# Seven half-size products for the first matrix product of two more groups, with a new schedule

## Chip, cores, metric

The kernel runs on one core of a Trainium2 chip. The metric is device microseconds from start to end of one execution. Three runs of the kernel before gave 276.33, 275.78 and 276.13 us: median **276.13 us**.

## What is computed

Linear attention with a positional weighting, and behind it a two-layer network with leaky ReLU. With B = 8 batches, H = 8 heads, S = 576 positions, D = 64:

```python
c, s = cos(pi/2 * pos/S), sin(pi/2 * pos/S)
phi(x) = concat(relu(x) * c, relu(x) * s)          # 128 features
kv  = einsum('bhsf,bhsd->bhfd', phi(k), v)
num = einsum('bhsf,bhfd->bhsd', phi(q), kv)
den = phi(q) . sum_s phi(k) + 1e-6
x   = (num / den) as 4608 tokens x 512
h   = x @ w_in                                      # 512 -> 2048
out = leaky_relu(h, 0.01) @ w_out                   # 2048 -> 512
```

Inputs and output are float32; the kernel multiplies in float16 and accumulates in float32.

## The kernel before, in words

**Groups.** The tokens go through the network in nine groups of 512: group g = 0 to 7 holds the first 512 positions of batch g, and group 8 the last 64 positions of all eight batches. For each group the kernel forms phi(q) (`q_prep`, tiles qp), transposes it by DMA (`q_transpose_dma`, qpT, line 363), and multiplies it with the batch's kv in four steps (`num`, line 400; PSUM pool ps_n with one buffer, which kv_sum uses too). Each num is divided on VectorE (DVE): den and its reciprocal (lines 411 and 415) and the product (line 416) into xs; line 377 then transposes the whole group by DMA into xT. Attention for batch b needs phi(k) (`k_cos` and `k_sin`, nine half-tiles each, written kp below, lines 251 on ScalarE (ACT) and 253 on DVE or GpSimd (POOL); kp has one buffer), v with a column of ones (`v_pairs`, vm), and `kv_sum` (72 small matmuls at line 326 and a copy on ACT at line 333).

**First product.** h = x @ w_in in two ways. *Direct* (`ffn1`, line 474, units "M"): 16 column blocks of 128, each four matmuls of 512 columns; ACT applies the leaky ReLU to two blocks at once (line 484, 128x1024). *By seven* (`ffn1s`, line 626, digits 1 to 7): the matrices are cut into 2 x 2 blocks, and seven products of half size stand for eight (Winograd's form of Strassen's scheme). A group has four units u, each of seven products, each of four matmuls of 256 columns. It needs sums of blocks of the weights (`w1_sum`, W sums in tile wext, once) and of x (`x_sum`, X sums, per group; n = 3 in place). The products of a unit accumulate in three of four PSUM banks, A, E and B. `ffn1e` moves between them: b copies A to B after product 1, s and u copy E and B aside, z adds u to E, y adds s to B (both on DVE, line 526), and a, c, e, d are four leaky ReLUs (ACT, line 653). Capital letters B, S, U put a copy on DVE. The fourth bank lets a unit begin while the last one is read; a unit's B and E are banks that the unit before releases through its e and a.

**Second product.** out = g @ w_out, by seven from group 1 on (`ffn2s`, line 737, units "F"): 14 parts, each of two half-units of four matmuls of 256 columns. Its block sums of g are `g_sum` (S1, S2 in tile ext; n = 3, 4 in place), those of w_out `weight_sum` (T), all on DVE. The results leave as osb on DVE or ACT and are stored from SyncE's queue (SP, line 796). Group 0's results are held and stored later (`store_held`, line 809).

**Order.** From batch 2 on, the order is written out in the table TUNE. Time is counted in units: stage g, positions 16g to 16g+16, holds ffn2 of group g and ffn1 of group g+1. `O[g+1]` is the order of the matmul units in that stage, spread evenly over it; everything else stands at a position, and each engine executes in that order. For batch b: `L` loads of q, k and v, `q`, `kc`, `ks`, `v` the phi and v steps with engines `e` (D, A, P; S is a POOL tensor_scalar in place of a cast), `qT` and `x` the two kinds of transposes, `mm` kv_sum and `n` the four nums. `S` and `S4s` are g sums, `W`, `X` and `T` the other sums, with engines `We` and `Xe`.

**Buffers.** Loads take a ring of four staging buffers (`stage_tile`), some of them tiles wext and ext: wext holds a quarter of w_in, then k of batch 1, then k of batch 3, before the W sums may use it. All loads, transposes and most stores are issued from SP in program order, so one that waits holds those behind it.

Seven-product ffn1 is in use for groups 4 to 8 (`F7 = 4`); groups 0 to 3 are direct.

Of the kernel before, what the change touches and what calls it, by code (L numbers as in the profile page):

```python
# [16 lines left out]
T = 9  # L17
# [3 lines left out]
def kernel(  # L21
# [15 lines left out]
    B, H, S, D = q.shape  # L37
# [12 lines left out]
    NG = B + 1  # L50
    NE = D + 2
    G7 = 1
    F7 = 4

    ctx.enter_context(tc.manual_schedule())

# [31 lines left out]
    def need(*keys):  # L88
        for key in keys:
            assert key in done, key  # L90
# [8 lines left out]


    wext = const.tile([P, 3080], dt.float32, name="wext")
    in_wext = {("w1", 1), ("k", 1), ("k", 3)}

    def stage_tile(nm, i, a, b, d):
        if (nm, i) in in_wext:
# [43 lines left out]
    w1 = {}  # L149
# [95 lines left out]
    kv = [const.tile([P, H, NE], dt.float16, name=f"kv{b}") for b in range(B)]  # L245
# [319 lines left out]
        )  # L565

    def w1_sum(bp, n, eng):
        need(("kv", 3), *(("W", bp, i) for i in {1: (), 2: (1,), 4: (2,), 3: (1,)}[n]))
        if n == 3:
            need(*(("f1", F7 - 1, 8 * bp + 4 + i) for i in range(4)))  # L570
        done.add(("W", bp, n))
        a11, a12, a21, a22 = (w1_quarter(bp, r, d) for r in range(2) for d in range(2))
        o1, o2, o4 = (SW[i][:, bp] for i in (1, 2, 4))
        if n == 1:
            tt_op(o1, a21, a22, ALU.add, eng)
        elif n == 2:
            tt_op(o2, o1, a11, ALU.subtract, eng)
        elif n == 3:
            tt_op(a21, a11, a21, ALU.subtract, eng)
        else:  # L580
            tt_op(o4, a12, o2, ALU.subtract, eng)
# [223 lines left out]
    held = []  # L805
# [24 lines left out]
    for hg in range(2):  # L830
        for j in range(J):
            e = ACT if j == 3 else POOL if hg == 1 and j == 2 else DVE
# [158 lines left out]
    for m in range(6):  # L991
# [4 lines left out]
    units = []  # L996

    TUNE = {'B': {2: {'L': None,
               'e': 'DDPDAPDDDAPPPDAPAPDDDADP',
               'kc': [13.8758, 13.8602, 13.7361, 13.8137, 13.7827, 13.8913, 13.7206, 14.2749, 13.7516],  # L1000
               'ks': [13.9533, 13.9378, 13.9068, 13.9223, 13.8292, 13.7671, 13.9844, 13.7051, 13.6896],
               'mm': 16.1999,
               'n': [17.3726, 19.1324, 20.1999, 21.6217],
               'q': [10.2124, 10.3249, 10.4374, 10.6624],
               'qT': [13.8447, 13.9689],
               'v': [10.5499, 13.5965],
               'x': 21.7526},
           3: {'L': [10.7749, 13.5654, 13.643, 19.8363],
               'e': 'AADDPAPAAADAAAAAPDAPPDAP',
               'kc': [18.9921, 17.2908, 19.2259, 23.109, 18.3817, 21.589, 20.6044, 16.9272, 21.5563],  # L1010
               'ks': [20.1181, 20.5226, 21.7199, 20.5635, 19.0389, 17.209, 19.0856, 20.6454, 20.4817],
               'mm': 23.4726,
               'n': [24.1999, 26.3817, 27.4726, 28.1454],
               'q': [19.1791, 20.6863, 15.7749, 22.6635],
               'qT': [20.9272, 22.7454],
               'v': [21.5235, 21.6544],
               'x': 28.2544},
           4: {'L': [16.5635, 25.2363, 22.8272, 22.8272],
               'e': 'PPAPDADDDPDDDAPADAAPPPPA',
               'kc': [36.3363, 36.0635, 37.2908, 33.1926, 33.3235, 38.7999, 28.5635, 36.2544, 37.6544],  # L1020
               'ks': [36.1181, 37.7363, 38.6908, 35.4181, 36.1726, 36.309, 36.0908, 38.3817, 36.9272],
               'mm': 38.9999,
               'n': [39.7817, 41.2581, 42.4144, 43.4726],
               'q': [21.7854, 22.3817, 33.2581, 34.3817],
               'qT': [28.6454, 36.1454],
               'v': [25.6544, 32.5963],
               'x': 43.7817},
           5: {'L': [33.6544, 32.9817, 36.2272, 36.2272],
               'e': 'ADADADADPDAADDDPPAADDAPA',
               'kc': [39.1635, 46.3272, 40.9817, 50.1825, 50.3564, 45.9363, 39.109, 46.0181, 45.6872],  # L1030
               'ks': [42.2835, 41.3235, 39.0544, 49.9695, 44.9817, 40.8726, 50.0086, 51.9216, 46.4363],
               'mm': 52.9651,
               'n': [53.6608, 55.9216, 55.0856, 58.1564],
               'q': [39.2181, 43.8908, 42.349, 45.2363],
               'qT': [44.8726, 50.7434],
               'v': [50.6651, 43.3908],
               'x': 58.7042},
           6: {'L': [41.389, 46.0999, 52.2695, 52.2695],
               'e': 'PPDAPAADPAPAPAPDDDADAPAD',
               'kc': [55.7086, 58.2086, 60.8173, 62.3042, 60.9495, 55.7869, 62.3303, 61.4869, 54.9962],  # L1040
               'ks': [55.0185, 60.9182, 60.7651, 57.139, 55.0409, 61.0121, 55.0633, 61.8086, 54.5303],
               'mm': 64.9495,
               'n': [66.9042, 68.5782, 70.7042, 74.5042],
               'q': [55.108, 59.0521, 55.7477, 61.8608],
               'qT': [59.1999, 64.4042],
               'v': [58.5303, 61.139],
               'x': 74.7042},
           7: {'L': [58.3564, 62.4086, 65.0121, 65.0121],
               'e': 'APPAAPDAAPAADPPAPAPAPPDA',
               'kc': [69.9695, 77.4869, 73.6999, 67.9216, 70.0477, 64.9808, 74.7434, 68.6173, 69.8608],  # L1050
               'ks': [78.7199, 65.9825, 70.8782, 69.3129, 78.6886, 65.4608, 73.6216, 69.8086, 68.6564],
               'mm': 81.0121,
               'n': [81.4869, 84.0956, 85.4869, 87.026],
               'q': [64.4434, 64.9182, 68.2695, 74.5564],
               'qT': [74.1825, 80.9025],
               'v': [75.0521, 76.6173],
               'x': 89.4869},
           8: {'L': [66.0347, 80.9182, 80.9495, 84.8173],
               'e': 'DAPD',
               'kc': [],  # L1060
               'ks': [],
               'mm': 10.1345,
               'n': [92.7912, 99.0521, 101.8347, 104.0956],
               'q': [80.9964, 84.7651, 85.139, 90.0086],
               'qT': [85.8347, 97.4869],
               'v': [],
               'x': 104.7912}},
     'O': {1: 'MMMMMMMMMM',
           2: 'FFFFFFFFFFFFFFFFFFFFFFFFFFFMMMMMMMMMFMMMMMMM',
           3: 'FMMFFFMFMFFFFFFFFFFFFFFMFMMMMMMMFFMFFMFMMFFF',  # L1070
           4: '1b5sFF6u3Fz2Fe1Fb7FFyFa56Uc2sF7ay4dF3FFz4e1FF5bFsdF362cuFz17FyeaFFF5bc64FsuFF3FF7zy2FFdace4d',
           5: '1bF5sFF63uF172Fzebay652uasF74cFy3dFzcF1FFe4b5FF6FsF23dU7azFyFe51FFbsFF23F6uFc47adzycFFFe4dFF',
           6: '1b5F1Fs6FuF327yzFFaFF5e4b2Fsc6FUF3zdF71yaF54eFb6Us32FzdcFaeFFF7y1bF5F6Fc2UF7asyc3F4dFzFe4dFF',
           7: '1b5F6S2F31FUzFeFFbF7a26u5ycF7sFaFyF45F3FFzSFde14bd26Uc3zFFF17eFyb6au25Fa47scy3dcFFFFFzFe4dFF',
           8: '1b5sFFFF2613u7FaFz5eFyFFbc4S6U2FF73ydaFz5c4FdFe1bFsFF632u17zFyFeFabF6Fu5c72s4y3zdaceFFFF4dFF',
           9: 'FFFFFFFFFFFFFFFFFFFFFFFFFFFF'},
     'S': {1: [13.612, 13.6585, 20.2817, 13.7982, 18.0181, 20.4408],
           2: [28.4817, 32.4654, 32.6617, 32.5308, 32.8726, 36.1999],
           3: [43.5544, 45.3454, 52.7912, 46.7454, 46.6635, 50.0477],
           4: [62.7042, 64.4825, 70.0086, 62.3825, 65.3129, 66.8521, 71.9216],  # L1080
           5: [81.0277, 81.1651, 82.8521, 78.6573, 81.1129, 82.9042, 85.6608],
           6: [91.3999, 92.6434, 100.6173, 92.5912, 97.1651, 99.7738, 97.1129],
           7: [108.6173, 113.8086, 117.8608, 113.4608, 113.5129, 113.8608, 117.8086],
           8: [124.939, 124.9912, 130.6856, 126.0086, 130.5142, 131.1713, 131.7428]},
     'S4': 21.6872,
     'S4s': {2: [37.5726, 41.1926],
             3: [59.2521, 60.0956],
             4: [74.6651, 73.6608],
             5: [87.5738, 87.0782],
             6: [106.7042, 103.5738],  # L1090
             7: [124.2695, 121.139]},
     'T': [10.8874, 13.5809, 13.674, 15.2749],
     'W': [[25.3454, 33.389, 36.2817, 42.4799], [35.5272, 39.8908, 40.1999, 50.5303]],
     'We': ['PDDP', 'DDDD'],
     'X': {4: [45.5563, 45.6217, 50.7042, 45.7526],
           5: [60.9808, 62.8782, 65.5129, 62.3564],
           6: [78.7512, 80.9338, 80.9808, 80.9651],
           7: [92.9651, 94.0086, 99.7216, 94.1825],
           8: [108.4434, 109.4869, 115.226, 109.6608]},
     'Xe': {4: 'DDDD', 5: 'PDDD', 6: 'DPDD', 7: 'DPDD', 8: 'PDDP'},  # L1100
     'held': 13.6275}

    for g in range(NG):
        order, seen = TUNE["O"][g + 1], {}
# [101 lines left out]
```

## Time and profile before

| | before |
|---|---|
| median of three runs | 276.13 us |
| the profiled execution, its own time | 276.87 us |
| its span | 275.1 us |
| TensorE (PE) busy, weight loads (PEld) | 266.3 us, 212.5 us |
| DVE, ACT, POOL busy | 201.5, 171.6, 112.2 us |
| bytes moved by DMA | 57.59 MB, 209 GB/s |

By stretches of the profiled execution (us busy):

| stretch, us | PE | PEld | DVE | ACT | POOL | DMA share |
|---|---|---|---|---|---|---|
| 53 to 66: direct ffn1 of group 1 | 13.00 of 13 | 7.06 | 12.93 | 9.58 | 11.34 | 1.12 |
| 66 to 92: ffn2 of group 1, group 2 begins | 24.98 of 26 | 18.98 | 18.38 | 14.12 | 19.53 | 0.95 |
| 92 to 125 | 33.00 of 33 | 22.25 | 23.39 | 23.55 | 17.66 | 1.04 |
| 125 to 160 | 34.77 of 35 | 32.58 | 29.62 | 26.98 | 21.79 | 1.01 |
| 160 to 193 | 32.70 of 33 | 30.73 | 27.62 | 24.61 | 15.08 | 0.70 |
| 225 to 257 | 32.00 of 32 | 30.18 | 23.16 | 20.43 | 2.31 | 0.21 |

How to read it: a line of the costliest groups gives the source line, engine and operation, what is written and read, the tile's shape, the count, then busy time and mean duration of one, then the engine's idle time ahead of them and what ended it. In the chain of waits and the order of time a line begins with start and duration in us. Matmuls overlap each other, so their mean duration is not their price. An engine's own durations overlap too, by about 0.1 us; from start to start is the price in a full queue.

### The profile page before, as it was taken

How to read it: one execution, taken by the hardware profiler on the slowest of the kernel's cores; microseconds unless marked ns; L12 is line 12 of the kernel's file. 1: busy time of each engine (PE TensorE's matmuls, PEld its weight loads, DVE VectorE, ACT ScalarE, POOL GpSimd, SP SyncE). 2: the span in 40 equal slices, each digit the busy share in tenths (PEclk: the TensorE clock that was granted, in tenths of full speed). 3: DMA queues.
4: the chain of work that ended last, by engine and by line, in shares of the span. 5: the costliest groups of instructions: out<-in, count | busy, mean ns of one | idle time of the engine just before them, and what ended most of it. 6: DMA issues, size and time to landing. Idle time of an engine off the chain costs nothing.

```text
span 275.1 us, 6879 instructions
## 1 busy us (share of the span) xinstructions
PE 266.3 (97%) x2813; PEld 212.5 (77%) x2813; DVE 201.5 (73%) x413; ACT 171.6 (62%) x293; POOL 112.2 (41%) x89
## 2 busy tenths in 40 slices
PE   8899999999999999999999999999999999999993
PEld 3575455557875568668999989999999999999983
DVE  4850597799964467888798878798997787667852
ACT  7756447478914476875679988756844565656400
POOL 2586002795679890440397899210510003000000
PEclk9999999999999999999999999999999999999999
DMA  7999999999699999989988997647915142211214
GB/s 223 373 393 411 383 399 370 374 365 231 207 162 245 302 218 254 289 234 231 226 293 125 272 234 208 148 114 159 183 48 128 27 101 67 69 38 40 77 44 111
DMA packets 77119, 57.59 MB, mean 209 GB/s; under 512 B 49312, under 2 KB 65696, under 8 KB 76704
## 3 DMA queue, kind: packets, MB, share of 16 engines
q1 hardware_dynamic: 76480, 56.63, 75.1%
q10 hardware_dynamic: 608, 0.52, 0.6%
q8 instruction: 22, 0.36, 0.5%
q14 instruction: 9, 0.07, 0.1%
HBM read 36.70 MB, written 9.44 MB: 168 GB/s over the span
## 4 chain that ended last, share of the span: by engine, by line
PE 78%; DMA 9%; DVE 5%; SPq 2%; POOL 2%; ACT 1%; issue 1%; ACTq 0%; DVEq 0%
PE ps L737 27%; PE ps_h L474 20%; PE ps_f L626 18%; PE ps_o L500 5%; DMA xT<-xs 4%; DMA kst<-in_k_dram 3%; PE ps_kv L326 2%; PE ps_num L400 2%; DMA qtl<-in_q_dram 2%; PE ps_f L737 1%; DVE ext L526 1%; POOL kp L253 1%; DVE xs L416 1%; SPq L363 1%; PE ps_qt L386 1%
## 5 line engine op out<-in xcount | busy, mean ns | idle before, releaser
L737 PEld LDWEIGHTS <-g 128*128 128x128 f16 x640 | 61.5, 98 | 8.3 <-DVE g L526 0.2
L737 PE MATMUL ps<-w,g 128*128 128x256 f16 x496 | 64.7, 273 | 0.1
L474 PE MATMUL ps_h<-xT,w 128*128 128x512 f16 (+1 forms) x272 | 59.0, 366 | 0.7 <-DMA xT<-xs 0.7
L474 PEld LDWEIGHTS <-w 128*128 128x128 f16 x272 | 30.0, 114 | 21.8 <-issue 0.8
L484 ACT ACTIVATE g<-ps_h 128x1024 f16<-128x1024 f32 x32 | 32.2, 1022 | 23.2 <-PE ps_h L474 23.1
L653 ACT ACTIVATE g<-ps_f 128x512 f16<-128x512 f32 x60 | 34.7, 596 | 12.9 <-DVE ps_f L526 6.2
L626 PEld LDWEIGHTS <-w 128*128 128x128 f16 x320 | 34.7, 114 | 0.8 <-issue 0.2
L626 PE MATMUL ps_f<-xT,w 128*128 128x256 f16 x240 | 34.4, 273 | 0.0
L737 PE MATMUL ps<-T,ext 128*128 128x256 f16 x240 | 31.4, 273 | 0.0
L253 POOL TENSOR_SCALAR kp<-kst,sin_t 128x256 f16<-128x256 f32 x16 | 20.6, 1295 | 21.7 <-PE ps_kv L326 21.7
L737 PEld LDWEIGHTS <-ext 128*128 128x128 f16 x256 | 24.7, 98 | 3.3
L626 PEld LDWEIGHTS <-wext 128*128 128x128 f16 x240 | 26.2, 114 | 1.2 <-issue 0.6
L253 POOL TENSOR_SCALAR qp<-qst,cos_t 128x512 f16<-128x512 f32 (+1 forms) x9 | 18.3, 2030 | 8.3 <-DMA qst<-in_q_dram 4.3
L416 DVE TENSOR_TENSOR xs<-ps_num,rden 128x512 f16<-128x512 f32 x28 | 19.4, 691 | 2.9 <-DMA xT<-xs 2.0
L253 POOL TENSOR_SCALAR kp<-kst,cos_t 128x256 f16<-128x256 f32 (+1 forms) x15 | 19.7, 1313 | 3.5 <-DMA kst<-in_k_dram 3.3
L626 PE MATMUL ps_f<-X,wext 128*128 128x256 f16 x128 | 18.9, 273 | 0.5 <-ACT ps_f L259 0.5
L526 DVE TENSOR_TENSOR osb<-ps,ext 128x512 f32<-128x512 f32 x23 | 15.7, 684 | 4.0 <-PE ps L737 3.4
L253 POOL TENSOR_SCALAR qp<-qst,sin_t 128x512 f16<-128x512 f32 (+1 forms) x9 | 18.3, 2036 | 0.0
L526 DVE TENSOR_TENSOR ext<-g 128x512 f16<-128x512 f16 (+1 forms) x23 | 14.2, 621 | 5.2 <-ACT g L484 3.4
L526 DVE TENSOR_TENSOR ps_f<-ps_f,u 128x512 f32<-128x512 f32 x20 | 13.9, 694 | 5.2 <-PE ps_f L626 2.7
L737 PE MATMUL ps<-ext,g 128*128 128x256 f16 x128 | 17.3, 273 | 0.0
L526 DVE TENSOR_TENSOR y<-ps_f,s 128x512 f32<-128x512 f32 x20 | 13.7, 687 | 3.2 <-PE ps_f L626 1.5
(118 smaller groups left out, 427.7 us busy)
## 6 DMA issues: line engine op xcount, KB each, us to landing
out_dram<-osb SPq DMA_DIRECT2D x32, 256.0 KB, 3.1
qst<-in_q_dram SPq DMA_DIRECT2D x7, 1024.0 KB, 10.3
kst<-in_k_dram SPq DMA_DIRECT2D x5, 1152.0 KB, 8.1
vst<-in_v_dram SPq DMA_DIRECT2D x5, 1152.0 KB, 7.1
w2st<-in_moe_w_out_dram SPq DMA_DIRECT2D x3, 1024.0 KB, 12.7
vst<-in_v_dram SPq DMA_DIRECT2D x4, 576.0 KB, 7.4
ext<-in_moe_w_in_dram SPq DMA_DIRECT2D x4, 512.0 KB, 10.3
kst<-in_k_dram SPq DMA_DIRECT2D x2, 576.0 KB, 8.1
```

What stands on the lines that cost most here:

```text
L253: eng.tensor_scalar(out=o, in0=i, scalar1=0.0, scalar2=col, op0=ALU.max, op1=ALU.mult)
L326: nc.tensor.matmul(ps[:, o, (c - lo) * NE : (c - lo + 1) * NE], lhsT=st["kp", b][sl, c, j, :], rhs=vm[sl, c, j, :], start=(j == 0), stop=( ...
L363: nc.sync.dma_start_transpose(out=qpT_pair(g, jp).rearrange("p o h t -> p (o h) t"), in_=st["qp2", g, jp].rearrange("p o h f -> p (o h f)"),)
L400: nc.tensor.matmul(ps[lo:hi, h // 4, (h % 4) * NE : (h % 4 + 1) * NE], lhsT=qpT[:, h, lo:hi], rhs=kv[b][:, h, :],)
L416: nc.vector.tensor_tensor(out=xs, in0=ps[:, :, 0 : 4 * NE].rearrange("p a (b e) -> p a b e", e=NE)[:, :, :, 0:D], in1=rden.rearrange("p (a ...
L474: nc.tensor.matmul(ps[:, m % 2, lo:hi], lhsT=w1[m // 4, c][0][:, w1[m // 4, c][1], m % 4 : 512 : 4], rhs=xT[:, lo // P : hi // P, c, :], s ...
L484: nc.scalar.activation(st["g", g][:, m - 1 : m + 1, :], ps, AF.Lrelu)
L500: nc.tensor.matmul(st["ps_o", g, tt], lhsT=st["g", g][:, m, tt * P : (tt + 1) * P], rhs=w2[:, m, :], start=(m == 0), stop=(m == NFT - 1),)
L526: eng.tensor_tensor(out=o, in0=a, in1=b, op=op)
L626: nc.tensor.matmul(ps[:, mi * HT : (mi + 1) * HT], lhsT=a[:, c, 2 * r0 + mi : 512 : 4], rhs=b[:, c], start=(n in (1, 5) and mi == 0 and c ...
L653: nc.scalar.activation(st["g", g][:, m : m + 2, r * HT : (r + 1) * HT], {"a": A, "c": y22, "e": E, "d": B_}[e].rearrange("p (m t) -> p m t ...
L737: nc.tensor.matmul(ps[:, tt], lhsT=a[:, i, tt * P : (tt + 1) * P], rhs=b[:, i], start=(first and i == 0), stop=(i == NPR - 1 and (apart or ...
```

## The change

Groups 2 and 3 also take the seven-product form (`F7 = 2`). The W sums may then begin once kv of batch 1 is summed, and wext no longer holds k of batch 3, which takes a staging buffer. The two g sums of groups 2 and 3 are cut as those of the later groups are. TUNE is replaced from batch 2 on: its core follows, with the lines for batches 2 and 3, the first stages and the first sums; positions, engines and orders for all later batches are other numbers of the same kind.

```diff
-    F7 = 4
+    F7 = 2
...
-    in_wext = {("w1", 1), ("k", 1), ("k", 3)}
+    in_wext = {("w1", 1), ("k", 1)}
...
     def w1_sum(bp, n, eng):
-        need(("kv", 3), ...
+        need(("kv", 1), ...
...
     TUNE 'B': 2:
-               'e': 'DDPDAPDDDAPPPDAPAPDDDADP',
-               'mm': 16.1999,
-               'n': [17.3726, 19.1324, 20.1999, 21.6217],
-               'q': [10.2124, 10.3249, 10.4374, 10.6624],
-               'qT': [13.8447, 13.9689],
-               'v': [10.5499, 13.5965],
-               'x': 21.7526},
+               'e': 'DPADPPDDDAPPAPPPPDDAAADD',
+               'mm': 16.4903,
+               'n': [16.8471, 17.2973, 17.6608, 17.8235],
+               'q': [10.1642, 10.8713, 10.357, 10.6785],
+               'qT': [14.2074, 14.2299],
+               'v': [10.4856, 14.1399],
+               'x': 17.8459},
     3:
-          {'L': [10.7749, 13.5654, 13.643, 19.8363],
-               'e': 'AADDPAPAAADAAAAAPDAPPDAP',
-               'mm': 23.4726,
-               'n': [24.1999, 26.3817, 27.4726, 28.1454],
-               'x': 28.2544},
+          {'L': [14.1174, 14.6999, 16.5912, 17.3599],
+               'e': 'AAAAAPAAPAAAAADPAAAPDDAA',
+               'mm': 19.3738,
+               'n': [21.3129, 22.7042, 24.6173, 25.6608],
+               'x': 26.5042},
...
      'O':
-           2: 'FFFFFFFFFFFFFFFFFFFFFFFFFFFMMMMMMMMMFMMMMMMM',
-           3: 'FMMFFFMFMFFFFFFFFFFFFFFMFMMMMMMMFFMFFMFMMFFF',
+           2: 'FFFFFFFFFFFFFFFFFFFF151bs63u2zae7Fybc5S624u3az75dyF1SFe4cb632duz7y1a5ebF6s4cuFF73d2Fy4zcaeFd',
+           3: 'F15F1bFs6FF2FFaF3uFz5FFFe7bySc62Ua34zdFe51b7yF62SuFa74F3dzc1F5FebyFFsFc6uFF347dzyF2FaeFFFc4d',
...
-     'W': [[25.3454, 33.389, 36.2817, 42.4799], [35.5272, 39.8908, 40.1999, 50.5303]],
-     'We': ['PDDP', 'DDDD'],
-     'X': {4: ..., 8: ...},
+     'W': [[10.4213, 13.2749, 17.8682, 18.8625], [10.2928, 10.5499, 10.807, 23.9216]],
+     'We': ['DDPP', 'PDDP'],
+     'X': {2: [19.426, 19.9216, 20.0956, 19.7477],
+           3: [31.1999, 31.2521, 33.8347, 33.339], ...},
-     'held': 13.6275}
+     'held': 10.7428}
```

In the new order of SP, the held stores come ahead of q of batch 3; both transposes of batch 2's q come next, then k of batch 3, the first half of its v, q of batch 4, a store, the second half of v and the transpose of group 2.

## Prediction

> **What bounds the kernel now.** I read the page's header and costliest groups first, then TensorE's (PE's) order of time around the first products of group 2, then the chain of waits there, then VectorE's (DVE's) order of time in the same stretch, and DMA issue to landing for single loads.
>
> ```profile
> span 275.1 us, 6879 instructions
> ...
> PE 266.3 (97%) x2813; PEld 212.5 (77%) x2813; DVE 201.5 (73%) x413; ACT 171.6 (62%) x293; POOL 112.2 (41%) x89
> ...
> L474 PE MATMUL ps_h<-xT,w 128*128 128x512 f16 (+1 forms) x272 | 59.0, 366 | 0.7 <-DMA xT<-xs 0.7
> ...
> L626 PE MATMUL ps_f<-xT,w 128*128 128x256 f16 x240 | 34.4, 273 | 0.0
> ```
>
> PE is busy 97% of the span with the clock at 0.9 or more in every slice: fewer PE cycles are worth their full time, unless PE waits instead. The means, 366 and 273 ns, are latencies of pipelined matmuls; the price is the spacing, and the chain of waits gives it:
>
> ```profile
> 77.04 5.39 DMA xT<-xs
> 82.43 0.04 issue
> 82.47 1.89 PE ps_h L474 x8
> 84.36 0.25 PE ps_num L400 x8
> ...
> 97.66 0.44 PE ps L737 x4
> 98.09 1.73 PE ps_h L474 x8
> ```
>
> Eight 512-column matmuls follow each other in 1.73 us, **216 ns each**; four of 256 columns in 0.44 us, **109 ns** (72 in a row at 257.69 take 7.86). The same lines show where PE does wait: the first product of group 2 (82.47) starts when the transpose xT of group 2 lands, 5.39 us after its issue at 77.04. That issue follows the fourth division of group 2 on DVE.
>
> **Matmuls.** The order of the changed kernel has 128 fewer L474 matmuls (two groups of 16 x 4) and 224 more at L626 (two groups of 4 units x 7 products x 4). Removed: 128 x 0.216 = 27.65 us. Added: 224 x 0.1092 = 24.48 us. **Sum -3.17 us**, all on PE. The weight loads at L626 (mean 114 ns, longer than 109) lie under the matmuls: the 240 matmuls of L626 show 0.0 us idle.
>
> This is where a page of the Trainium skill speaks against the change: TensorE: Matmul & The Clock Gate, section Back-to-back issue gap, gives 131 ns for each 512-column matmul in a sustained stream. By that, the removed ones were worth 16.8 us and the change would lose 7.7 us on PE; the trace has 216 ns, so the measurement decides.
>
> **Where the gain can be lost: the start of group 2's products.** Before, 27 half-units of ffn2 (4 matmuls each) and one num step of group 3 stand on PE between the start of this stage (65.16) and the first product. After, 20 half-units and no num of group 3. So 7 x 0.437 + 0.26 = 3.32 us of work moves behind the first product. The work behind it is then 3.32 - 3.17 = **+0.15 us** against before. In other words: if the first product starts at the same 82.47, nothing is gained; a gain needs it up to 3.3 us earlier. I follow what it waits for.
>
> ```profile
> 52.65 0.48 DVE L253 TENSOR_SCALAR qp<-qst,cos_t 128x512 f16<-128x512 f32 x1
> ...
> 60.42 0.77 DVE L526 TENSOR_TENSOR ext<-ext,g 128x1024 f16<-128x1024 f16 x1
> ...
> 66.77 0.43 DVE L526 TENSOR_TENSOR ext<-g 128x512 f16<-128x512 f16 x1 [0.49 <-ACT g L484]
> ...
> 68.71 0.17 DVE L411 TENSOR_SCALAR den<-ps_num 128x8 f32<-128x8 f32 x1
> 68.92 0.20 DVE L415 RECIPROCAL rden<-den 128x8 f32<-128x8 f32 x1
> 69.15 0.69 DVE L416 TENSOR_TENSOR xs<-ps_num,rden 128x512 f16<-128x512 f32 x1
> 69.76 0.42 DVE L526 TENSOR_TENSOR ext<-ext,g 128x512 f16<-128x512 f16 x1
> ```
>
> DVE is full from 52.65 to the first division of group 2, save 0.49 us. Up to 67.57 (before two qp of batch 3) it works 14.43 us. In the new order this list loses two qp (0.64 each, start to start) and two kp (0.35), and gains a vm half (0.67), four W sums of 1024 (as the ext sum at 60.42: 0.70 each, 2.8), one 512 sum (0.35) and the g sums that stood after the third division (1.20): 14.43 - 1.28 - 0.70 + 0.67 + 2.80 + 0.35 + 1.20 = 17.5 us, so the first division can start at 70.1. Five kp of batch 2 stand 2.25 us ahead of that and end at 67.9; kv_sum(2) needs them and PE reaches it at 66.5 (65.16 + three half-units). On ACT the kp of batch 2 end about 67.1, behind the last two g of group 1; POOL has eight kp at 1.14 to 2.04 us from about 52.8, to 62 or 69 (66 at the 1.67 of its six rows there before). **kv_sum(2) starts at 67.9, 1.4 us late**, and runs 1.25.
>
> From there: num 0 at 70.05 (8 matmuls and the kv copy between), its division 0.45 later for 1.13 us, done 71.65. The nums share one PSUM buffer, so each waits for the division ahead. In the new places only 12, 8 and 4 matmuls stand between them (1.31, 0.87, 0.44 us), with one osb sum in DVE's way: num 1 at 71.7, its division done 73.6; num 2 73.65, done 75.2; num 3 75.25, done 76.85. Issue of the transpose at 76.85 (77.04 before), plus 5.39: **xT lands at 82.25**. From one side, the median landing is 4.6 us (81.5); from the other 6.25 us at group 5 (83.1), because half of batch 3's v (71.66 before) is now issued just ahead of it on SP, behind a store that waits for the osb sum.
>
> Beside it, kv_sum(3) also stands before the first product, and its input comes later than before: k of batch 3 no longer goes into wext at 46.66 but into a stage buffer, behind the held stores (49.33 to 52.93), q of batch 3 and both transposes of batch 2's q. The second of these needs a DVE qp that ends near 59 in the new list; at 2.4 us per issue k starts at about 62 and, with 6.7 to 8.1 us to landing, is there at 69 to 70, where kp must wait for kv_sum(2) anyway (69.15). ACT then has kv and t1 copies, eleven kp, six qp halves and both vm halves: 1.1 + 11 x 0.40 + 6 x 0.62 + 2 x 1.05 = 11.3 us from 69.3, done 80.6. kv_sum(3) ends at about 81.9: just inside xT. So the first product starts at **82.3, against 82.47: -0.2 us** (from 80.7, if DVE's list is 1.6 shorter or the landing faster, to 84, if v lands late).
>
> **The dense stage behind it.** From there 28 products, 7 half-units and 4 nums are 16.4 us on PE, 4.1 per unit. Before, the g of this group needed eight ACT instructions of 1.02 us and no DVE. Now ACT has 26 evacuations (two copies take 1.07 us, 0.53 each) = 13.8 us and 1.6 of qp and kp: 15.4. DVE has eight y and z and two s (0.65), four divisions (1.13), two X (0.45) and five other sums and a vm: about 15.3. Later units, in before from group 4 on, stand among one ffn2 half-unit per product (some 6.1 us each) and run almost without PE idle; here they are packed closer than any row shows. The chain in one unit, b copy 0.58, product 0.44, u copy 0.59, z 0.69, e 0.60, is 2.9 us plus four handovers, about 3.4, under 4.1. Lower end 0 us; upper end, if each unit finds one division (1.13) in its way and ACT runs over by another 1.2, 4 x 0.4 + 1.2 = 2.9. I take **+1.2**, nearer the lower end, since both engines still fit.
>
> **What costs nothing.** The X sums of groups 2 and 3: 2 us per group on DVE and POOL, inside the dense stage's sum or under a full PE stage. W sums moved earlier: counted on DVE; on POOL one of 2.12 us ahead of qp, covered until 66. Two vm halves (batches 5 and 6) become a POOL tensor_scalar of 1152 elements: between the cast's 1.2 us and 4.8 (from 2.13 us per 512), off the path while POOL has slack there (41% of the span). Group 3's products stand among ffn2 as the later groups' do. The remaining stages are set anew; their PE idle before is under 1 us in all (0.7 of it one xT wait at 159.6), so -0.6 to +1.5, taken as 0.
>
> **Sum** against the profiled execution (276.87 us, span 275.1): -0.2 + 0.15 + 1.2 = +1.15. The median of the runs shown is 276.13, 0.74 below; **276.13 + 1.15 = 277.3 us**.
>
> **Rivals.** (1) *The chain is shorter, and the gain comes through.* It decides at the first product: break-even is a start at 81.1 with the dense stage as taken, 82.3 with none of its cost. With the transpose at 4.6 us and DVE 1 us ahead it starts at 80.5: -2.0 + 0.15 + 0.4 = -1.4, 274.7; with no waits at all the full -3.17, 273.0. For it: PE would be ready at 77.5 (65.16 + 20 half-units, four nums, two kv_sums), and many ends lie within a microsecond of each other; against: DVE, ACT and a transpose must all be early. Chance 0.33. (2) *Evacuation becomes the bound*: v of batch 3 late and dense units held by ACT and DVE: start at 84 (+1.5), dense +2.9: +4.5, 280.7. For it: ACT's 26 evacuations where 8 stood; against: no engine's sum exceeds PE's time. Chance 0.14. (3) *Weight loads no longer hide*, so that each matmul of the two groups pays its 114 ns as well: -3.17 + (224 - 128) x 0.114 = +7.8 us, 283.9; the L626 row's 0.0 idle speaks against. Chance 0.01. That it does not do what it says is out: the order has the counts.
>
> On (3), the Trainium skill, TensorE: Matmul & The Clock Gate, Part 3 (The mechanism), says weight loads overlap running matmuls only in other row groups; the trace disagrees, as L626 spaces full-array matmuls at 109 ns with loads of 114.
>
> **Numbers.** Forecast +1.15, chance 0.52, its own range 275.7 to 278.8; (1) 0.33, (2) 0.14, (3) 0.01. A difference under 0.2% (0.55 us) can't be told from none. Faster: 0.31 of (1) and 0.04 of the forecast's lower end, 0.35. Same: 0.02 and 0.12, 0.14. Slower 0.51. The range, 273.8 to 280.6, reaches most of (1) and (2).
>
> **What would show it.** Right: L626 with 784 matmuls at 109 ns; the first L626 matmul of group 2 at 82 to 83, released by xT or kv_sum(3); a DVE row ending PE's wait ahead of kv_sum(2); 1 to 2 us of PE idle between 82 and 100. Wrong: first product before 81, or the dense stage without idle (then rival 1), or ACT rows as releasers of several us (rival 2), or new idle after 100.

## The result and the profile after

| | before | after |
|---|---|---|
| median of six runs each | 275.89 us (275.65 to 276.33) | **278.16 us** (277.36 to 279.98) |
| the profiled execution, its own time | 276.87 us | 277.36 us |
| its span | 275.1 us | 275.5 us |

The changed kernel is slower by 2.3 us: ratio **1.0083, 95% interval 1.0059 to 1.0106**. The two profiled executions differ by only 0.5 us, for the one of before lies above all six of its runs and the one of after is the fastest of its six. In the experiments, medians are over all executions, and ratios leave out the few that lie over 1.5% above the fastest of their kernel.

The header of the page of after, and two rows of its costliest groups with shapes kept apart:

```profile
span 275.5 us, 7171 instructions
...
PE 264.1 (96%) x2909; PEld 222.3 (81%) x2909; DVE 216.3 (79%) x425; ACT 186.7 (68%) x337; POOL 126.2 (46%) x101
...
L626 PE MATMUL ps_f<-xT,w 128*128 128x256 f16 x336 | 48.7, 273 | 1.8 <-DMA xT<-xs 1.8
...
L474 PE MATMUL ps_h<-xT,w 128*128 128x512 f16 x112 | 24.9, 379 | 0.1
```

L474 has 128 matmuls fewer (112 of this shape and 32 of another), L626 has 784 in its five rows, and all but 0.1 us of the idle time ahead of them is the 1.8 us in this row. The saved PE work is real; PE waits instead. PE's order of time, from the first num of batch 2 to the first product of group 2 (start, duration, what; in brackets the idle time ahead and what ended it):

```profile
69.35 0.42 PE L400 MATMUL ps_num<-kv,qpT 128*128 128x66 f16 x8
...
70.99 0.43 PE L400 MATMUL ps_num<-kv,qpT 128*128 128x66 f16 x8
...
73.04 0.41 PE L400 MATMUL ps_num<-kv,qpT 128*128 128x66 f16 x8 [0.75 <-DVE xs L416]
...
74.68 0.43 PE L400 MATMUL ps_num<-kv,qpT 128*128 128x66 f16 x8 [0.79 <-DVE xs L416]
...
79.91 0.75 PE L326 MATMUL ps_kv<-vm,kp 64*128 64x66 f16 x36 [0.20 <-ACT vm L259]
82.49 0.63 PE L626 MATMUL ps_f<-xT,w 128*128 128x256 f16 x4 [1.83 <-DMA xT<-xs]
```

The nums are 1.64, 2.05 and 1.64 us apart, each waiting for the division ahead of it (`xs`). The transpose is issued at 76.30, xT lands 6.14 us later, and the first product starts at 82.49, where the first product before started at 82.47. From 20 us on, PE's waits of over 0.15 us (start to start, less the spacing of that kind of matmul) sum to 2.8 us before and 6.3 us after: 3.5 us of new waits against 3.17 us of saved work, which makes up nearly all of the 0.4 us between the spans. Of the waits, 1.5 us before and 4.7 us after lie between 60 us and the first product. So nothing is gained in the profiled pair. It does not yet explain 2.3 us between medians: 1.0 us of them is that the profiled execution of before was that much slower than its median, and 0.8 us that the one of after was faster than its own.

### The profile page after: what moved, and what is told of

It reads as the page before. It is cut to its first block, busy times and chain, and to the rows that moved or that the text cites. A ratio compares the mean times of both kernels' runs of the same rounds, so it can differ in the third digit from the quotient of the medians.

```text
span 275.5 us, 7171 instructions
## 1 busy us (share of the span) xinstructions
PE 264.1 (96%) x2909; PEld 222.3 (81%) x2909; DVE 216.3 (79%) x425; ACT 186.7 (68%) x337; POOL 126.2 (46%) x101
## 4 chain that ended last, share of the span: by engine, by line
PE 82%; DMA 5%; ACT 4%; DVE 4%; issue 1%; POOL 1%; SPq 1%; DVEq 0%; ACTq 0%
PE ps L737 30%; PE ps_f L626 29%; PE ps_h L474 10%; PE ps_o L500 5%; DMA kst<-in_k_dram 3%; PE ps_num L400 3%; PE ps_kv L326 3%; DMA xT<-xs 2%; ACT g L653 2%; PE ps_f L737 1%; POOL kp L253 1%; DVE ext L526 1%; ACT kp L251 1%; DVE xs L416 1%; DVE osb L526 1%
## 5 line engine op out<-in xcount | busy, mean ns | idle before, releaser
L653 ACT ACTIVATE g<-ps_f 128x512 f16<-128x512 f32 x84 | 48.0, 597 | 17.9 <-DVE ps_f L526 10.1
L626 PEld LDWEIGHTS <-w 128*128 128x128 f16 x448 | 48.7, 114 | 2.7 <-DMA xT<-xs 1.9
L626 PE MATMUL ps_f<-xT,w 128*128 128x256 f16 x336 | 48.7, 273 | 1.8 <-DMA xT<-xs 1.8
L626 PEld LDWEIGHTS <-wext 128*128 128x128 f16 x336 | 36.6, 114 | 1.1 <-issue 0.2
L253 POOL TENSOR_SCALAR kp<-kst,cos_t 128x256 f16<-128x256 f32 (+1 forms) x24 | 31.5, 1320 | 9.3 <-DVE s L261 6.1
L474 PE MATMUL ps_h<-xT,w 128*128 128x512 f16 (+1 forms) x144 | 28.9, 355 | 0.1
L626 PE MATMUL ps_f<-X,wext 128*128 128x256 f16 x176 | 26.3, 273 | 0.1
L474 PEld LDWEIGHTS <-w 128*128 128x128 f16 x144 | 15.9, 114 | 10.8 <-issue 0.2
L653 ACT ACTIVATE g<-y 128x512 f16<-128x512 f32 x28 | 17.7, 634 | 5.4 <-DVE y L526 5.4
L484 ACT ACTIVATE g<-ps_h 128x1024 f16<-128x1024 f32 x16 | 15.9, 1023 | 7.0 <-PE ps_h L474 7.0
L259 ACT COPY ps_f<-ps_f 128x512 f32<-128x512 f32 x26 | 14.9, 573 | 6.9 <-PE ps_f L626 6.4
L253 POOL TENSOR_SCALAR qp<-qst,cos_t 128x512 f16<-128x512 f32 (+1 forms) x6 | 11.3, 1890 | 14.8 <-DMA qpT<-qp 6.4
```

The source lines that it names most:

```text
L253: eng.tensor_scalar(out=o, in0=i, scalar1=0.0, scalar2=col, op0=ALU.max, op1=ALU.mult)
L259: nc.scalar.copy(o, i)
L474: nc.tensor.matmul(ps[:, m % 2, lo:hi], lhsT=w1[m // 4, c][0][:, w1[m // 4, c][1], m % 4 : 512 : 4], rhs=xT[:, lo // P : hi // P, c, :], s ...
L484: nc.scalar.activation(st["g", g][:, m - 1 : m + 1, :], ps, AF.Lrelu)
L626: nc.tensor.matmul(ps[:, mi * HT : (mi + 1) * HT], lhsT=a[:, c, 2 * r0 + mi : 512 : 4], rhs=b[:, c], start=(n in (1, 5) and mi == 0 and c ...
L653: nc.scalar.activation(st["g", g][:, m : m + 2, r * HT : (r + 1) * HT], {"a": A, "c": y22, "e": E, "d": B_}[e].rearrange("p (m t) -> p m t ...
```

## Experiments

Twelve runs, one of them the changed kernel again, each timed beside before, whose median was 276.06 to 276.22 us there. Theories: **A**, the chain to the first product (nums in one PSUM buffer, division, transpose) sets the loss; **B**, the dense stage of group 2 is bound by ACT and DVE; **C**, the new plan of the later stages is worse; **D**, a wait of 2 us lets PE's clock fall; and further down **E**, **F** and **G**.

### 1. The changed kernel again, and four half-units moved ahead

`a_again` is the changed kernel. `a_fill4` moves four half-units of ffn2 from among group 2's products to ahead of them:

```diff
- 2: 'FFFFFFFFFFFFFFFFFFFF151bs63u2zae7Fybc5S624u3az75dyF1SFe4cb...
+ 2: 'FFFFFFFFFFFFFFFFFFFFFFFF151bs63u2zae7ybc5S624u3az75dy1Se4cb...
```

> The changed kernel once more, unchanged, for a second profiled execution: its first profile (own time 277.36 us) is the fastest of six runs (277.36 to 279.98). Theory A (the start of group 2's products is set by the division and transpose chain, which holds DMA landings): a slower execution shows its extra time ahead of the first product of group 2, first product at 83 to 85 instead of 82.49, and the stretch behind it as long as in the first profile (193.0 us to the span's end). Rival C (the newly set later stages vary): first product at 82.5 and more PE waits behind 100 us.

Measured: 278.47 us, ratio 1.0084 (1.0058 to 1.0110). The profiled execution of this run (span 277.5) has its first product at the same 82.48, but then something that the profile of after lacks. Busy time by stretches, `a_again`; the column behind POOL is the granted clock:

```profile
80.00:82.00 2.00, 0.40 (x25) 0.27 (x17) 0.23 (x1) 0.60 (x1) 0.00 (x0) 1.00 1.68 49
82.00:84.00 2.00, 1.51 (x8) 1.07 (x9) 0.85 (x2) 0.44 (x1) 1.03 (x1) 0.60 1.09 245
84.00:86.00 2.00, 2.00 (x12) 1.42 (x11) 0.00 (x0) 0.72 (x2) 2.00 (x3) 0.54 1.17 239
```

and the same stretches of after:

```profile
82.00:84.00 2.00, 1.51 (x14) 1.52 (x15) 0.85 (x2) 0.85 (x2) 1.02 (x1) 1.00 1.10 247
84.00:86.00 2.00, 2.00 (x26) 1.95 (x25) 0.83 (x3) 1.47 (x4) 2.00 (x3) 1.00 1.17 250
```

PE is busy for the same time and does 20 matmuls instead of 40: behind the wait for xT the clock is halved for 3.41 us, and the first num of batch 3 starts at 86.73 instead of 85.15: **1.6 us lost**. Part of D is shown. A's sign, a first product at 83 to 85 us, did not come, and of C's, more waits behind 100 us, only 0.4 us.

> Four ffn2 half-units (1.75 us of PE) moved from among group 2's products to ahead of them, where PE waited 1.83 us for xT. Theory A: the first product still starts at about 82.5, the work behind it is 1.75 us less, so the time falls by 1.0 to 1.75 us against the changed kernel. Rival B (evacuation by ACT and DVE bounds the dense stage): the stage takes as long as before with four half-units less, first products of group 3 no earlier, time unchanged within 0.4 us.

Measured: 278.97 us, ratio 1.0114 (1.0086 to 1.0142). PE has hardly a wait ahead of the first product (82.29) and no fall of the clock, but in the dense stage of `a_fill4`:

```profile
86.16 0.43 PE L400 MATMUL ps_num<-kv,qpT 128*128 128x66 f16 x8 [0.35 <-DVE xs L416]
87.99 0.60 PE L626 MATMUL ps_f<-X,wext 128*128 128x256 f16 x4 [0.97 <-ACT ps_f L259]
...
93.56 0.60 PE L626 MATMUL ps_f<-X,wext 128*128 128x256 f16 x4 [0.55 <-ACT ps_f L259]
96.85 0.60 PE L626 MATMUL ps_f<-X,wext 128*128 128x256 f16 x4 [0.50 <-ACT ps_f L259]
```

3.8 us of waits from 85 to 97 us, start to start, mostly for ACT's copies (L259). The time is 0.5 us above that of the changed kernel beside it, near B's price, not 1.0 to 1.75 us below. So the change left seven half-units of cover in the dense stage, and with four of them out B holds. These four can't be shifted from here to fill the wait.

### 2. Two PSUM buffers for the nums

```diff
-            at(t["n"][j], num, b, j)
+            at(t["n"][j], num, b, j, "h" if b == 2 and j % 2 else "n")
```

In `a_num2buf` nums 1 and 3 of batch 2 take a buffer of pool h instead of the one of pool n; `b_num2buf` is the same edit in the kernel before.

> Nums 1 and 3 of batch 2 write to the other PSUM pool, so no num waits for the division ahead of it (PE waited 0.75 and 0.79 us for them). Theory A: the divisions follow each other on DVE without gaps, the transpose issues at about 75.2 instead of 76.3, the first product starts at about 81.3, and the time falls by 0.8 to 1.2 us; the PE wait ahead of the first product grows to about 2.5 us. Rival (each PE wait taken away is gained by itself): 1.5 us or more. Rival B: first product earlier but no gain.

Measured: 276.27 us, ratio to before **1.0007 (0.9985 to 1.0029)**: 2.2 us less than the changed kernel beside it (`a_again`). The nums now start at 69.09, 70.65, 71.78 and 72.69, the transpose is issued at 74.73 instead of 76.30, and the first product starts at 80.34. That is more than A's price of 0.8 to 1.2 us and fits the rival's, 1.5 us or more. Part of it is a landing: xT came 4.53 us after its issue, where it took 6.14 in after, and with 6.14 it would have come at 80.87, 0.5 us too late for this first product. Now the inputs of kv_sum of batch 3 are late; PE's order of time of `a_num2buf`:

```profile
78.50 0.81 PE L326 MATMUL ps_kv<-vm,kp 64*128 64x66 f16 x34 [1.09 <-DVE kp L253]
79.66 0.75 PE L326 MATMUL ps_kv<-vm,kp 64*128 64x66 f16 x36 [0.35 <-ACT vm L259]
```

In this execution too the clock was halved, from 80.42 us on for 3.41 us.

> The kernel before with nums 1 and 3 of batch 2 in the other PSUM pool, so that the gain of that edit in the changed kernel can be told from one that has nothing to do with the change. Theory A: before, the nums stand further apart and PE waits 0.24 us for one division; DVE works without a gap ahead of the transpose, so the time stays within 0.3 us of the kernel before. Rival (the single buffer delays the transpose in both kernels): 1 us faster.

Measured: 275.85 us, ratio 0.9995 (0.9979 to 1.0011). In before the single buffer costs nothing that can be told from noise (the interval is -0.6 to +0.3 us); there PE has 3.3 us more work to do before the first product. So A holds in both kernels, if not in its price: the edit that is worth 2.2 us in the changed kernel is worth nothing in the old one.

### 3. Keeping PE busy through the wait

`a_warm` adds eight matmuls of 512 columns whose result nothing uses, between kv_sum of batch 3 and the first product; `a_num2buf_warm` has them ahead of that kv_sum, and the two buffers.

```diff
+    def keep_warm(n):
+        ps = psum("h", [P, MAIN], dt.float32, "ps_warm")
+        for _ in range(n):
+            nc.tensor.matmul(ps, lhsT=ident, rhs=w2[:, 0, :])
+    at(19.42, keep_warm, 8)
```

> The changed kernel with eight matmuls of 512 columns (1.73 us, their result is used by nothing) between kv_sum of batch 3 and the first product of group 2, where PE waited 1.83 and 2.26 us for xT in the two profiles. Theory D (the wait lets the granted clock fall, to 0.54 to 0.60 between 82 and 86 us in the second profile, 1.6 us lost in some executions): no fall of the clock there, median 277.2 to 277.6, spread under 1 us. Rival (the spread of 277.4 to 280 comes from DMA landings): median 278.3, spread as before, first product at different times. If the matmuls are in the way: 278.5 or more.

> Nums 1 and 3 of batch 2 in the other PSUM pool, and the same eight matmuls ahead of kv_sum of batch 3, where PE then waited 1.28 and 0.53 us for vm. Theory D: no fall of the clock at 81 to 85 us, which cost the profile of the two-buffer kernel 1.66 us between first product and the first num of batch 3 (4.32 us instead of 2.66): 274.3 to 274.9, faster than the kernel before. Rival: as without them, 276.3.

Measured: 279.13 us, ratio 1.0085 (1.0055 to 1.0116), and 276.63 us, 1.0018 (1.0000 to 1.0035). In neither profile does the clock fall, and neither kernel is faster for it: the ratio of `a_warm` stands for 278.4 us, as much as the changed kernel's. So D is not the whole of it. These runs weigh less than they seem to. Two of the six executions of `a_warm` have a mean clock of 0.993 all the same (281.81 and 281.50 us), and in the profile of `a_num2buf_warm` xT landed 6.76 us after its issue, so that the first product came at 81.88, 1.5 us later than in `a_num2buf`. The profile of `a_warm` shows another loss, 35 us later; its chain of waits:

```profile
108.05 9.90 DMA qpT<-qp
117.94 0.05 issue
117.99 0.43 PE ps_num L400 x8
```

The second transpose of batch 4's q landed 9.90 us after its issue, and PE waited 2.6 us for it.

### 4. That transpose earlier, and kv_sum as cover

`a_qT` moves it ahead of the load that it stood behind. `a_kvlate` has that, the two buffers, three half-units moved ahead, and kv_sum of batch 3 behind the third product.

```diff
   B 4:  -'q': [.., 33.6216], 'qT': [30.1825, 35.2416]
         +'q': [.., 33.13],   'qT': [30.1825, 33.21]
   (a_kvlate also:)  B 3:  -'mm': 19.3738   +'mm': 20.45
                     O 2:  three F moved to the front
```

> The changed kernel, with one edit: the last qp of batch 4 and the second transpose of its q are put earlier, so that the transpose is issued ahead of the load of q of batch 5 (106.11 us after the changed kernel's profile, behind that load). Theory D (what the medians lose beyond the profiled 0.4 us is the half clock behind the wait for the first product): nothing changes, 278.3 us, executions 277.4 to 279.5. Rival E (this transpose has too little margin, and its late landing, 2.61 us of PE wait in the profile with the eight unused matmuls, is what spreads the executions): 277.5 us, all executions within 1 us of each other.

Measured: 279.03 us, ratio 1.0093 (1.0065 to 1.0120), 277.36 to 280.88. The transpose now lands 5.19 us after its issue and PE doesn't wait for it, but E falls: it is not what spreads the executions of the changed kernel.

> The changed kernel with two PSUM buffers for the nums of batch 2, the earlier transpose as in the run beside this one, three half-units of ffn2 moved ahead of group 2's first product, and kv_sum of batch 3 (1.25 us of matmuls) moved from ahead of that product to behind the third one. Theory A (the loss is PE's wait ahead of the first product: with two buffers alone 1.81 us, for the inputs of kv_sum of batch 3, and for xT): PE reaches the first product at about 78.5, xT lands at about 79.2, so a wait of 0.7 us, too short for the clock to fall, and kv_sum finds its inputs ready: 276.3 - 1.1 = 275.2 us, and executions close together, 274.7 to 276; faster than before by 0.3%. Rival B (the dense stage is bound by evacuation, so what is gained ahead of it is lost inside it, as with the four half-units moved): waits of 1 us and more between 80 and 97, 276.3 us as with two buffers alone.

Measured: 281.77 us, ratio 1.0181 (1.0137 to 1.0225), the worst of the two-buffer kernels. PE's order of time of `a_kvlate`:

```profile
80.26 0.63 PE L626 MATMUL ps_f<-xT,w 128*128 128x256 f16 x4 [1.57 <-DMA xT<-xs]
...
84.19 0.60 PE L626 MATMUL ps_f<-X,wext 128*128 128x256 f16 x4 [1.18 <-ACT ps_f L259]
...
88.62 0.60 PE L626 MATMUL ps_f<-X,wext 128*128 128x256 f16 x4 [0.96 <-ACT ps_f L259]
...
93.47 0.60 PE L626 MATMUL ps_f<-X,w 128*128 128x256 f16 x4 [1.38 <-DVE y L526]
```

Rival B again, and more than its price: 5 us of waits from 82 to 95. The first of them is the edit's own: kv_sum and its copy now stand ahead of the b copy of the first unit on ACT, which executes in order.

### 5. The inputs of that kv_sum, and the load ahead of the transpose

`a_kvin`: two buffers, and kp of batch 3 ahead of other sums. `a_vearly`: two buffers, and the second half of v of batch 3 loaded 7 us earlier.

```diff
   (a_kvin:)    B 3:  kc[2] from A to P;  ks[3] from A to D, 19.1869 -> 18.95
                S4: 18.2086 -> 19.0;  W[0][3]: 18.8625 -> 19.3
   (a_vearly:)  B 3:  'L': [14.1174, 14.6999, 16.5912, 17.3599 -> 16.60]
```

> The changed kernel with two PSUM buffers for the nums of batch 2, and with the inputs of kv_sum of batch 3 brought forward and nothing moved on PE: a g sum of 2048 on DVE (2.38 us) and a W sum on POOL (2.12 us) go behind the kp of batch 3 that they stood ahead of, and two of ACT's kp go to DVE and POOL. Theory A (PE's waits between the nums of batch 2 and group 2's first product are the loss; with two buffers alone 1.28 us for a kp on DVE and 0.53 us for the second vm half): the first wait goes, the second stays at 0.5, then 0.3 us for xT; first product 1 us earlier, no fall of the clock in most executions: 275.4 us, 0.25% faster than before. Rival B (what is gained there is lost inside the dense stage, to the copies and leaky ReLUs of ACT and the sums of DVE, as with kv_sum moved): 276.2 us, as with two buffers alone, and new waits of 0.5 us and more between 80 and 97.

Measured: 277.45 us, ratio 1.0053 (1.0030 to 1.0077); neither theory's time. The kp are earlier, as planned, and yet the first product came at 82.07 in the profiled execution, 1.77 us after kv_sum, because xT itself landed 6.71 us after its issue at 75.31; and the clock fell, as by the mean clock (0.994 or less) it did in eight of the twelve executions. A's remaining gain needs a transpose that lands early, and that was not so here.

> The changed kernel with two PSUM buffers for the nums of batch 2, and with the load of the second half of batch 3's v put right behind the first half, some 7 us earlier, instead of right ahead of the transpose of group 2 (in the changed kernel's profile 72.33, and the transpose 76.30 with 6.14 us to landing; 6.1 to 6.8 us in most profiles of its variants, 5.39 before). Theory F (the load in flight is what lengthens the transpose): xT lands 5.4 us or less after its issue, the second vm half and with it kv_sum of batch 3 are bound by ACT's list as before, first product at 80.3 at the latest, fewer executions with a half clock: 275.7 us. Rival G (the transposes of q that are issued right behind it share its engines and lengthen it): 6 us and more as now in some executions, 276.3 us as with two buffers alone.

Measured: 276.48 us, ratio 1.0006 (0.9986 to 1.0026). In its profile xT landed 4.46 us after its issue and is not what the first product waits for (80.27, right behind kv_sum). But `a_num2buf`, with the load where it was, had 4.53 and 80.34. So the trace doesn't show that this half load (576 KB, issued 2.7 us ahead of the transpose there and 4.0 in after) lengthens the transpose; F's gain does not come, and the time is that of the two buffers alone.

### 6. Group 3 alone

`g3_only` and `g3_fix`: `F7 = 3`, with the first stages of before (its batches 2 and 3, the order of stage 1, and its sums) and the later ones of after; the W sums, which need k of batch 3 gone from wext, all on DVE in stages 1 and 2.

```diff
-    F7 = 2          in_wext = {("w1", 1), ("k", 1)}
+    F7 = 3          in_wext = {("w1", 1), ("k", 1), ("k", 3)}
-    'W': [[10.4, 13.3, 17.9, 18.9], [10.3, 10.5, 10.8, 23.9]]
+    'W': [[24.3, 25.1, 27.0, 31.95], [26.3, 27.3, 28.9, 38.0]]
   (g3_fix also:)  batch 4's loads at the positions of before
```

> The change done for group 3 alone: group 2 direct again, with the kernel before's places and order for batches 2 and 3, stages 0 and 1 and their sums; the changed kernel's places from batch 4 and stage 2 on; W sums placed between 24 and 32. Theory A: group 3's products start amid ffn2 work with no transpose to wait for, so its 1.6 us are gained: 274.0 to 275.0 against 275.9 of the kernel before. Rival C (the newly set later stages lose): no faster than before, 275.9 or more.

Measured: 281.81 us, ratio 1.0200 (1.0173 to 1.0227). This one was marred by its own edit: with the loads of after, the whole v of batch 4 (1152 KB) is issued at 76.23, right ahead of the transpose of group 2. The transpose itself is issued in time, at 77.10 (77.04 in before), but lands late:

```profile
77.10 8.68 DMA xT<-xs
```

So PE waited 4.20 us up to 85.83, and the clock was halved for two periods, 6.83 us. `g3_fix` moves that load away.

> Group 3 alone by seven products again, with the kernel before's places for the loads of batch 4: in the first try the load of v of batch 4 stood ahead of the transpose of group 2 on SP and waited for a buffer that POOL's qp of batch 3 held, so that PE waited 4.4 us and the clock fell. Theory A: group 3's products stand among ffn2 work, so its 1.6 us are gained: 274.2 to 275.2. Rival C (the newly set later stages lose what is gained): 275.9 or more.

Measured: 277.37 us, ratio 1.0051 (1.0031 to 1.0072). The transpose, issued at 77.12 without the load ahead of it, lands after 5.50 us: the wait for a buffer that the expectation names is not what had made PE wait, the landing is. Half the saved work, and no gain either; C's price (275.9 or more) came. The largest wait of the profile is for a sum on DVE:

```profile
104.75 1.48 PE L737 MATMUL ps<-T,ext 128*128 128x256 f16 x12 [1.67 <-DVE ext L526]
```

DVE works without a gap ahead of that sum, but only since 98.00. Before, it stood idle, because the X sum of group 3, next in its order, waited for xT; DVE's order of time:

```profile
98.00 0.43 DVE L526 TENSOR_TENSOR X1b<-xT 128x512 f16<-128x512 f16 x1 [4.39 <-DMA xT<-xs]
```

Whether the new later stages or the mix of two plans does this, these two runs don't tell.

### The clock, over all executions

Every execution's mean granted clock is recorded; 3.41 us at half speed lower it by 3.41 x 0.5 / 275 = 0.006. Of the twelve executions of the changed kernel (its six and those of `a_again`), four have 0.993 or 0.994, with a median of 279.38 us; the other eight have 0.996 or more and a median of 277.92. Of 97 executions of before, two have 0.994. So the half clock comes to one execution in three and costs it about 1.5 us, as in the trace. Of `a_fill4`, whose profile has next to no wait ahead of the first product (0.16 us), none of six executions has less than 0.997. But the eight at full clock are still 1.8 us above before, so the half clock is the smaller part of the 2.3 us.

When it falls can be read off five traces. The full-speed stretch ahead of it lasts 78.51 us (`a_again`, `a_qT`, `g3_only`) or 75.09 us (`a_num2buf`, `a_kvin`): 23 and 22 periods of 3.413 us. I counted PE's idle time, start to start less the spacing of that kind of matmul, in each such period. In the last one ahead of the fall it is 2.57, 2.67, 3.30, 2.07 and 2.49 us; in the worst ones that led to no fall, between 65 and 120 us, 2.01 (after), 2.00 (`a_kvlate`) and 1.87 us. A few ns more or less in the spacing move such a sum by some hundredths of a us, so 2.07 and 2.01 are hardly apart. The last wait of after, 2.0 us, is nearly as long as that of `a_again`, 2.26, but the end of a period cuts 0.46 us off it. The Trainium skill, TensorE: Matmul & The Clock Gate, Part 1: The HAM clock gate, describes a free-running window of 3413 ns, which the lengths of the stretches bear out. It also says that the clock falls after a window without work; in these traces some 2.1 us of idle time in 3.41 are enough.

## Why the prediction was right, and where it was not

**Direction and sum.** Forecast +1.15 us, measured +2.3 us between medians; slower, inside the range. The direction is in part luck. All of the forecast's slowdown was the dense stage's +1.2 us, which did not come; without it the sum says no change, as the profiled pair nearly shows. What made the medians slower was no term of the sum.

**Matmuls, -3.17 us: right** (224 x 0.1092 is 24.46, not 24.48; nothing hangs on it). 784 matmuls at L626, weight loads of 114 ns, and in after the first products follow each other at 0.44 us for four. The waits explain the rest without a price for weight loads; rival 3 is out.

**The start of group 2's products, -0.2 us: right in the end and in its mechanism, not in each link.** kv_sum of batch 2 was forecast at 67.9 and came at 67.22. No kp of DVE held it: the five ended at 67.06, so DVE's list was over-counted by 0.8 us. PE itself was late, since a half-unit ahead of kv_sum waited 0.5 us for the last g of group 1 on ACT. The nums were forecast 1.65, 1.95 and 1.60 us apart and came 1.64, 2.05 and 1.64 apart. The issue was forecast at 76.85 and came at 76.30; the landing, taken as 5.39 us, took 6.14. The two misses cancel by luck: 82.3 forecast, 82.49 measured. That one PSUM buffer sets this pace was argued there; `a_num2buf` shows it, with nums 1.56, 1.13 and 0.91 us apart. The kv_sum of batch 3 ended at 80.6 instead of 81.9 and did not matter in after.

**The dense stage, +1.2 us: mis-sized.** Busy time of after from the first product on (the length, then PE, weight loads, DVE, ACT and POOL, then the granted clock):

```profile
82.49:100.00 17.51, 17.41 (x179) 16.54 (x180) 15.00 (x31) 14.81 (x28) 14.29 (x10) 1.00 1.00 269
```

The stage costs 0.1 us by busy time and 0.4 us start to start, near the lower end of the range given: ACT and DVE were counted about right (15.4 and 15.3 us forecast, 14.8 and 15.0 measured) and fit beside PE. (The upper end of the range, 4 x 0.4 + 1.2, is 2.8 and not 2.9.) The prediction's sign of being right, 1 to 2 us of PE idle here, did not come, and its sign of rival 1, a dense stage without idle, nearly did without rival 1. But the stage has little slack: with four half-units less (`a_fill4`) it loses 3.8 us.

**The rest, 0 (-0.6 to +1.5): two costs that no term had.** In the profiled pair the rest was inside its range: waits of over 0.15 us behind 100 us sum to 0.9 us before and 0.5 us after. Other executions pay one or both of two costs in the place of the 1.2 us. First the *half clock*: the prediction saw PE's wait ahead of the first product and priced it as idle time alone, while it also costs 1.5 us in a third of the executions, 0.5 us in the mean. Second, *late q transposes in the later stages*. In the second profile of the changed kernel, `a_again`, ACT's order of time has a qp that waits for its buffer, still being read by a transpose:

```profile
167.53 0.72 ACT L251 ACTIVATE qp<-qst,cos_t 128x512 f16<-128x512 f32 x1 [0.68 <-DMA qpT<-qp]
```

and in `a_kvin` the chain of waits leads from such a transpose through this qp to PE, which waits 1.17 us:

```profile
153.89 14.34 DMA qpT<-qp
168.22 0.02 issue
...
171.06 1.03 PE ps_f L626 x8
```

In the kernels with the new later stages this transpose took 12.2 to 14.6 us from issue to landing, twelve traces in all; in before and `b_num2buf` it took 7.2 and 7.0. Up to 12.8 us PE loses nothing to it (12.73 in after); at 13.53 it loses 0.38 us (`a_again`), at 14.32 and 14.34 1.18 and 1.17 us (`a_vearly`, `a_kvin`), at 14.64 1.48 us (`a_qT`). So what the landing takes beyond some 13.15 us is lost one for one. It fits the spread of the eight executions at full clock, 277.36 to 278.69, but no trace of a slow one among them was kept. That C, the new later plan, makes the landing late is likely, since it did so too with group 2 direct (`g3_fix`, 12.57); it was not tried by itself and stays open.

**From the profiled execution to the median.** The prediction took 0.74 us off, since before's profiled execution lay that far above its median. It assumed that the changed kernel's runs would lie about their profile as before's do. They don't: the profiled one was the fastest of six. And the profile of before was a poor yardstick. That of `b_num2buf` (275.74 us, near before's median) has 2.0 us of waits where that of before has 2.8; set against it, after has 4.3 us of new waits for 3.17 us of saved work, a loss of 1.1 us in the profiled execution already (the spans differ by 1.5). Whether most executions of before look like that, no trace shows.

**Rival 1** (the chain is shorter) failed at the point that it named: the first product did not come before 81.1. With two buffers it does (80.34), and the time falls to that of before, not to the 274.7 that rival 1 priced. **Rival 2** is right as a mechanism wherever cover is taken away (`a_fill4`, `a_kvlate`), not in the kernel as changed.

No version beat the kernel before. In the profiles the 3.17 us of saved work come back as waits (1.5 us before, 4.7 after, from 60 us to the first product) at the one place where PE, done earlier, must stand still for a chain of num, division and transpose that did not become shorter.

## What to carry over

Before taking work off a full engine, look for the next point where that engine waits for a chain that runs elsewhere: work removed ahead of it only lengthens the wait, and one buffer in that chain was worth 2.2 us here, as much as the change had lost. Price a wait of TensorE of some 2 us and more with the half clock behind it, which came by chance here and so showed as spread. Profile more than one execution of a kernel before its profile is used as a yardstick. When work is moved to fill a wait, check what it covered at the place that it leaves.

## What the hardware showed beyond this

- The granted clock fell to 0.5 for exactly one or two periods of 3.41 us, on a grid whose place differs from execution to execution, once PE was idle for some 2.1 us or more of a period; 2.0 us did not do it (five falls).
- The DMA transpose xT of group 2 landed between 4.5 and 6.8 us after its issue, by execution and variant; it took 4.5 us with a half load of 576 KB 2.7 us ahead of it (`a_num2buf`) as without (`a_vearly`). With a whole load of 1152 KB issued 0.9 us ahead of it (`g3_only`) it took 8.7 us, and 5.5 us without (`g3_fix`). A qpT near 154 us took up to 14.6 us. What else sets the landing stays open.
- L626's full-array matmuls kept their spacing of 109 ns with weight loads of 114 ns (mean) through 784 matmuls of after.
